# New SBUF addresses for the operands of the feed-forward matmuls in a fused attention and feed-forward kernel

## The chip, the cores and the metric

The kernel runs on one core of one Trainium2 chip, in one launch. The metric is the device time of that launch in microseconds. Before the change it is 646.93 us, the median of three runs (645.04, 646.93 and 648.34).

## What is computed

The reference is an attention layer followed by a two-layer feed-forward network, all in float32. Batch 4, 8 heads, 768 positions, head size 64; 3072 tokens of width 512, inner width 2048. Each query sees its neighbours at a distance below 16 and 24 block summaries (the maximum of the keys and the mean of the values of each block of 32 positions).

```python
k_sum = k.reshape(B, H, nb, block, D).max(axis=3)
v_sum = v.reshape(B, H, nb, block, D).mean(axis=3)
scores_all = concat([where(|i - j| < 16, scale * q @ k.T, -1e9), scale * q @ k_sum.T + log(block)])
attn = softmax(scores_all) @ concat([v, v_sum])
x = attn.transpose(0, 2, 1, 3).reshape(B * S, H * D)
h = x @ w_in
g = h * tanh(softplus(h))
out = g @ w_out
```

## The kernel before, in words

**Tiling.** The tokens are cut into 6 groups `g` of 512, the inner width into 16 blocks `fc` of 128. A pair (g, fc) is a step, 96 in all. Every float32 operand of the feed-forward part is kept as two numbers of type fp32r, an upper part (`hi`, `xh`, `ah`) and a rest (`lo`, `xl`, `al`), and a product is the sum of three: upper by upper, rest by upper, upper by rest.

**The feed-forward matmuls.** `ff_in` (L416, its matmul at L422) makes one 128x512 block of `h`: the stationary operand is a 128x128 slice of `w_in`, the moving one a 128x512 slice of `xh` or `xl`; 4 slices times 3 products are 12 matmuls a step. `ff_act` (L426) applies the activation on ScalarE, `ff_split` (L432) makes `ah` and `al`. `ff_out` (L442, its matmul at L450) has a 128x128 slice of `ah` or `al` as stationary operand and a 128x512 slice of `w_out` as moving one: 4 token tiles times 3 products, 12 matmuls a step, added up over the 16 blocks in four PSUM banks. That makes 96 x 24 = 2304 matmuls of 512 columns. Each has a weight load of its own for its stationary operand.

**Weights.** They arrive as raw 64-bit words, are made into `hi` and `lo` on ScalarE and VectorE in the first part of the run, and stay in SBUF. Blocks 0 to 9 are the `w_early` tiles, taken from the pool `const` (L98 to L103). Blocks 10 to 15 are the `w_late` tiles, taken after the pool `first_att` (L161) has been given back (L583).

**Attention.** It has units of 64 queries x 4 of a pair of heads. Its matmuls are in float32: scores (L312 to L318), transposes of the probabilities (L371, moving operand `ident`, stationary `pr`), products with the values (L398, moving operand `pt`, stationary `vw`), and at the start sums of values (L247, moving `vw` or `v`, stationary `blocks`). They stand between the steps.

**What sets the order.** The first part follows a written list of operations (`order`, L541 on), the rest a loop over the steps (L606 on): `ff_in` of step i, attention work, `ff_out` of step i - 2. TensorE takes all its work in this order.

**What sets the addresses.** A pool's tiles lie one behind the other in SBUF, the pools in the order in which they are opened. Addresses below are bytes from the start of a partition. A slice of a stationary operand begins a multiple of 512 bytes behind its tile's start, a slice of a moving operand a multiple of 2048 bytes.

Of the kernel before, what the change touches and what calls it, by code (L numbers as in the profile page):

```python
# [10 lines left out]
F32R = mybir.dt.float32r  # L11
# [9 lines left out]
P = 128  # L21
# [8 lines left out]
HP = H // 2  # L30
NCC = DM // P
NFC = DFF // P
# [7 lines left out]
EARLY = 10  # L40
NR = (S - TG) // P
NW = CG * NQ
WP = 512
# [14 lines left out]
def fused_kernel(ctx: ExitStack, tc: tile.TileContext, q0, qk, kt, v0, vw, vs, w_in, w_out, out):  # L58
    nc = tc.nc
    PS = bass.MemoryType.PSUM  # L60

    const = ctx.enter_context(tc.tile_pool(name="const", bufs=1))
    stage = ctx.enter_context(tc.tile_pool(name="stage", bufs=2))
    xp = ctx.enter_context(tc.tile_pool(name="xp", bufs=2))
    att = ctx.enter_context(tc.tile_pool(name="att", bufs=2))
    small = ctx.enter_context(tc.tile_pool(name="small", bufs=8))
    ff = ctx.enter_context(tc.tile_pool(name="ff", bufs=3))
    ps_o = ctx.enter_context(tc.tile_pool(name="ps_o", bufs=4, space=PS))

    ps_w = ctx.enter_context(tc.tile_pool(name="ps_w", bufs=4, space=PS))  # L70
# [9 lines left out]
    for h in range(2):  # L80
        r = slice(h * QT, (h + 1) * QT)
        nc.gpsimd.affine_select(
            out=base[r, 0:KW], in_=base[r, 0:KW], pattern=[[1, KW]], base=-1,
            channel_multiplier=-1, compare_op=ALU.is_ge, fill=NEG / SCALE)
        nc.gpsimd.affine_select(
            out=base[r, 0:KW], in_=base[r, 0:KW], pattern=[[-1, KW]], base=2 * WIN - 1,
# [8 lines left out]
    nc.gpsimd.memset(last[QT:P, KW - WIN:KW], NEG / SCALE)  # L95


    def weight_tiles(pool, name, blocks):  # L98
        return [[pool.tile([P, blocks, WP], F32R, name=f"{name}_{w}_{part}") for part in ("hi", "lo")]
                for w in ("in", "out")]  # L100

    early = weight_tiles(const, "w_early", EARLY)
    late = []  # L103

    def weight(w, part, fc):
# [52 lines left out]


    begin = ExitStack()  # L160
    first_att = begin.enter_context(tc.tile_pool(name="first_att", bufs=HP))  # L161

    blocks = first_att.tile([P, NW + NR, NB], F32, tag="blocks", name="blocks", bufs=1)
    nc.gpsimd.memset(blocks, 1.0 / BLK)
    for part, step, at0 in ((blocks[:, :NW], QT, -WIN), (blocks[:, NW:], P, TG)):
        n = part.shape[1]
        nc.gpsimd.affine_select(
            out=part, in_=part, pattern=[[step, n], [-BLK, NB]], base=at0, channel_multiplier=1,  # L170
            compare_op=ALU.is_ge, fill=0.0)
        nc.gpsimd.affine_select(
            out=part, in_=part, pattern=[[-step, n], [BLK, NB]], base=BLK - 1 - at0, channel_multiplier=-1,
            compare_op=ALU.is_ge, fill=0.0)
    part = blocks[:, :NW]
    nc.gpsimd.affine_select(
        out=part, in_=part, pattern=[[0, NW], [0, NB]], base=-WIN, channel_multiplier=1,
        compare_op=ALU.is_ge, fill=0.0)
    nc.gpsimd.affine_select(
        out=part, in_=part, pattern=[[0, NW], [0, NB]], base=WIN + QT - 1, channel_multiplier=-1,  # L180
# [384 lines left out]
    def parse(word):  # L565
        name = next(m for m in sorted(ops, key=len, reverse=True) if word.startswith(m))
        return name, word[len(name):]
# [10 lines left out]
    for k, word in enumerate(order):  # L578
        name, what = parse(word)
        ops[name](what)  # L580
        if k == end_of_begin:
            begin.close()
            late += weight_tiles(ctx.enter_context(tc.tile_pool(name="late", bufs=1)), "w_late", NFC - EARLY)  # L583


    done = 1 + max(int(word[2:]) for word in order if word.startswith("ph"))
# [19 lines left out]
    for i in range(done, len(steps) + 2):  # L606
# [24 lines left out]
        if i in transposes:  # L631
            home = ff.tile([P, WB * WP], F32, tag="f", name=f"pt_{i}", bufs=1)[0:KA]
# [48 lines left out]
```

## Time and profile before

| what | before |
|---|---|
| device time, median of 3 runs | 646.93 us (645.04 to 648.34) |
| span of the profiled execution, first to last instruction | 645.3 us |
| TensorE busy, share of the span | 626.7 us, 97% |
| TensorE weight loads busy | 510.5 us, 79% |
| VectorE / ScalarE / GpSimd busy | 288.8 / 270.5 / 75.0 us |

The profiled execution has no time of its own beside its span; the span lies between the lowest and the middle one of the three runs. Matmuls are pipelined: the record of one goes on after the next has started, so a busy TensorE is not TensorE at its peak, and the step from one start to the next is shorter than a record.

### The profile page before, as it was taken

The numbers are of one execution on the slowest core, as the hardware profiler recorded it, in microseconds if no ns is written. First come the engines' busy times: TensorE is split into PE (matmuls) and PEld (weight loads), VectorE is DVE, ScalarE is ACT, GpSimd is POOL, SyncE is SP. The second block draws the span as 40 slices with busy tenths as digits, with TensorE's granted clock in tenths as the row PEclk, the third lists the DMA queues.
The fourth block names the chain that finished last, engine by engine and source line by source line (L and its number), as shares of the span: only waits on it lengthen the run. The fifth ranks groups of instructions, "written<-read, shape, count | busy, mean of one in ns | idle before, by whom it ended". The sixth has DMA issues, their size and how long they took to land.

```text
span 645.3 us, 10991 instructions
## 1 busy us (share of the span) xinstructions
PE 626.7 (97%) x4272; PEld 510.5 (79%) x4272; DVE 288.8 (45%) x817; ACT 270.5 (42%) x659; POOL 75.0 (12%) x119
## 2 busy tenths in 40 slices
PE   4799899999999999999999999999999999999997
PEld 3687788777888888888888888888888888888886
DVE  4899999993222445423223444332332232222211
ACT  4887678583433425415424434244244251111111
POOL 4432121220101001001001010010010010000000
PEclk9999999999999999999999999999999999999999
DMA  8978656642202234603202254233132010100001
GB/s 263 243 263 287 211 216 202 226 163 93 67 27 93 73 121 113 216 1 95 63 33 93 91 153 125 86 95 94 66 94 81 15 32 1 65 1 0 1 0 66
DMA packets 31780, 68.24 MB, mean 106 GB/s; under 512 B 6768, under 2 KB 11632, under 8 KB 31728
## 3 DMA queue, kind: packets, MB, share of 16 engines
q1 hardware_dynamic: 31728, 67.53, 33.2%
q8 instruction: 34, 0.56, 0.4%
q14 instruction: 18, 0.15, 0.1%
HBM read 59.11 MB, written 6.29 MB: 101 GB/s over the span
## 4 chain that ended last, share of the span: by engine, by line
PE 80%; DVE 6%; ACT 1%; issue 1%; DVEq 0%
PE po L450 37%; PE ph L422 36%; PE x_ps L398 3%; PE sc L312 2%; PE pt_ps L371 2%; DVE w L140 1%; DVE al L440 1%; DVE w L136 1%; DVE w_f L144 1%; DVE w_f L149 1%; DVE w_early_out_lo L157 1%; ACT pr L345 0%; DVE vq L260 0%; DVE km L239 0%; DVE pr L334 0%
## 5 line engine op out<-in xcount | busy, mean ns | idle before, releaser
L429 ACT ACTIVATE a<-ph 128x512 f32<-128x512 f32 x96 | 57.2, 597 | 250.5 <-PE ph L422 166.6
L438 DVE CAST ah<-a 128x512 fp32r<-128x512 f32 x80 | 34.1, 426 | 239.1 <-ACT a L429 237.7
L365 POOL TENSOR_TENSOR pr<-pr,rs 128x480 f32<-128x480 f32 x48 | 54.8, 1143 | 362.2 <-DVE rs L361 297.3
L450 PE MATMUL po<-w_early_out_hi,ah 128*128 128x512 f32 x240 | 96.6, 402 | 0.0
L450 PE MATMUL po<-w_early_out_hi,al 128*128 128x512 f32 x240 | 95.1, 396 | 0.1
L422 PE MATMUL ph<-xh,w_early_in_hi 128*128 128x512 f32 x240 | 95.1, 396 | 0.0
L450 PE MATMUL po<-w_early_out_lo,ah 128*128 128x512 f32 x240 | 94.6, 394 | 0.0
L422 PE MATMUL ph<-xh,w_early_in_lo 128*128 128x512 f32 x240 | 94.0, 392 | 0.0
L422 PE MATMUL ph<-xl,w_early_in_hi 128*128 128x512 f32 x240 | 93.6, 390 | 0.0
L345 ACT ACTIVATE pr<-pr,nm 128x120 f32<-128x120 f32 x192 | 73.3, 384 | 9.5 <-DVE nm L334 9.3
L440 DVE TENSOR_TENSOR al<-a,ah 128x512 fp32r<-128x512 f32 x96 | 68.1, 710 | 4.0 <-ACT ah L438 1.3
L422 PE MATMUL ph<-xh,w_late_in_hi 128*128 128x512 f32 x144 | 57.6, 400 | 0.0
L450 PE MATMUL po<-w_late_out_hi,ah 128*128 128x512 f32 x144 | 57.2, 397 | 0.0
L422 PE MATMUL ph<-xh,w_late_in_lo 128*128 128x512 f32 x144 | 57.0, 396 | 0.1
L422 PE MATMUL ph<-xl,w_late_in_hi 128*128 128x512 f32 x144 | 56.8, 394 | 0.0
L450 PE MATMUL po<-w_late_out_lo,ah 128*128 128x512 f32 x144 | 56.3, 391 | 0.0
L450 PE MATMUL po<-w_late_out_hi,al 128*128 128x512 f32 x144 | 56.2, 390 | 0.0
L450 PEld LDWEIGHTS po<-w_early_out_hi,ah 128*128 128x128 f32 x240 | 45.2, 188 | 11.6 <-issue 1.9
L450 PEld LDWEIGHTS po<-w_early_out_lo,ah 128*128 128x128 f32 x240 | 45.3, 189 | 10.6
L450 PEld LDWEIGHTS po<-w_early_out_hi,al 128*128 128x128 f32 x240 | 45.3, 189 | 10.4 <-DVE al L440 0.5
L422 PEld LDWEIGHTS ph<-xh,w_early_in_lo 128*128 128x128 f32 x240 | 45.1, 188 | 10.0
L422 PEld LDWEIGHTS ph<-xl,w_early_in_hi 128*128 128x128 f32 x240 | 45.2, 188 | 9.5
(77 smaller groups left out, 828.7 us busy)
## 6 DMA issues: line engine op xcount, KB each, us to landing
qk<-qk SPq DMA_DIRECT2D x40, 496.0 KB
w<-w_in SPq DMA_DIRECT2D x16, 512.0 KB
w<-w_out SPq DMA_DIRECT2D x16, 512.0 KB
vw<-vw SPq DMA_DIRECT2D x40, 192.0 KB
ks<-kt SPq DMA_DIRECT2D x16, 384.0 KB
out<-o SPq DMA_DIRECT2D x24, 256.0 KB
vsum<-vs SPq DMA_DIRECT2D x12, 384.0 KB
vw<-vm SPq DMA_DIRECT2D x40, 48.0 KB
```

Source lines behind the costliest of these rows:

```text
L136: nc.vector.tensor_scalar(out=x, in0=x, scalar1=29, scalar2=None, op0=ALU.logical_shift_right)
L140: nc.vector.scalar_tensor_tensor(out=x, in0=high, scalar=SIGN, in1=x, op0=ALU.bitwise_and, op1=ALU.bitwise_or)
L312: nc.tensor.matmul(ps[h][row, at0:at0 + KA], u["qk"][r, s, h * QT:(h + 1) * QT], u["qk"][r, s, P:], start=True, stop=True)
L345: nc.scalar.activation(pr[:, s, :], pr[:, s, :], AF.Exp, scale=-1.0, bias=nm[:, s:s + 1], accum_out=sm[:, s:s + 1])
L365: nc.gpsimd.tensor_mul(u["p"], u["p"], u["r"].unsqueeze(2).broadcast_to([P, NQ, KA]))
L371: nc.tensor.transpose(ps[:KA, s * P:(s + 1) * P], u["p"][:, s, :], ident)
L398: nc.tensor.matmul(x, u["v"][0:rows, s, d], pt, start=(c >= CG), stop=(c >= CG or s == NQ - 1))
L422: nc.tensor.matmul(ph, w[:, cc * P:(cc + 1) * P], x[:, cc, :], start=(cc == 0 and n == 0), stop=(cc == NCC - 1 and n == 2))
L429: nc.scalar.activation(a, st[g, fc], AF.Mish)
L438: (nc.scalar.copy if g == 0 else nc.vector.tensor_copy)(ah, a)
L440: return lambda: nc.vector.tensor_sub(al, a, ah.bitcast(F32))
L450: nc.tensor.matmul(po[g][t], a[:, tok], w, start=(fc == 0 and n == 0), stop=(fc == NFC - 1 and n == 2))
```

## The change

No operation, size or order changes. The pools get other places: `pool(name, bufs, side)` takes a pool's memory from the low end of SBUF (`left`) or from the high end (`right`). `ff` (with `ah`, `al`) and `const` (with `w_early_in`) come first from the low end; `xp` (`xh`, `xl`) and a new pool `moving` (with `w_early_out`) first from the high end.

```diff
-    const = ctx.enter_context(tc.tile_pool(name="const", bufs=1))
-    stage = ctx.enter_context(tc.tile_pool(name="stage", bufs=2))
-    xp = ctx.enter_context(tc.tile_pool(name="xp", bufs=2))
-    att = ctx.enter_context(tc.tile_pool(name="att", bufs=2))
-    small = ctx.enter_context(tc.tile_pool(name="small", bufs=8))
-    ff = ctx.enter_context(tc.tile_pool(name="ff", bufs=3))
+    def pool(name, bufs, side):
+        return ctx.enter_context(tc.tile_pool(name=name, bufs=bufs, side=side))
+
+    ff = pool("ff", 3, "left")
+    const = pool("const", 1, "left")
+    xp = pool("xp", 2, "right")
+    moving = pool("moving", 1, "right")
+    stage = pool("stage", 2, "right")
+    att = pool("att", 2, "right")
+    small = pool("small", 8, "right")
...
-    early = weight_tiles(const, "w_early", EARLY)
+    early = weight_tiles((const, moving), "w_early", EARLY)
...
-    first_att = begin.enter_context(tc.tile_pool(name="first_att", bufs=HP))
+    first_att = begin.enter_context(tc.tile_pool(name="first_att", bufs=HP, side="left"))
...
-            late += weight_tiles(ctx.enter_context(tc.tile_pool(name="late", bufs=1)), "w_late", NFC - EARLY)
+            late += weight_tiles([pool("late", 1, "left")] * 2, "w_late", NFC - EARLY)
```

`weight_tiles` takes one pool for `w_in` and one for `w_out`. In the two built programs the tiles of the feed-forward part begin here (bytes in the partition):

| tile | role | before | changed |
|---|---|---|---|
| w_early_in_hi, _lo | stationary in `ff_in` | 3104, 23584 | 23584, 44064 |
| w_late_in_hi, _lo | stationary in `ff_in` | 180128, 192416 | 64544, 76832 |
| xh (2 buffers) | moving in `ff_in` | 105504, 113696 | 196576, 204768 |
| xl (2 buffers) | moving in `ff_in` | 121888, 130080 | 212960, 221152 |
| ah (3 buffers) | stationary in `ff_out` | 167840, 169888, 171936 | 9344, 11392, 13440 |
| al (3 buffers) | stationary in `ff_out` | 173984, 176032, 178080 | 15488, 17536, 19584 |
| w_early_out_hi, _lo | moving in `ff_out` | 44064, 64544 | 155616, 176096 |
| w_late_out_hi, _lo | moving in `ff_out` | 204704, 216992 | 89120, 101408 |
| vw (2 buffers) | stationary at L398 | 152480, 154528 | 128736, 130784 |
| pt (first list / loop) | moving at L398 | 156576 / 159648 | 132832 / 1152 |
| ident | moving at L371 | 1152 | 21632 |

## Rows read from the trace of the kernel before

**Rows 1.** The page: span, and busy time by engine (share of the span, instructions).

```profile
span 645.3 us, 10991 instructions
PE 626.7 (97%) x4272; PEld 510.5 (79%) x4272; DVE 288.8 (45%) x817; ACT 270.5 (42%) x659; POOL 75.0 (12%) x119
```

**Rows 2.** The page's 40 slices: granted TensorE clock in tenths.

```profile
PEclk9999999999999999999999999999999999999999
```

**Rows 3.** The page: chain that ended last, by engine and by line.

```profile
PE 80%; DVE 6%; ACT 1%; issue 1%; DVEq 0%
PE po L450 37%; PE ph L422 36%; PE x_ps L398 3%; PE sc L312 2%; PE pt_ps L371 2%; DVE w L140 1%; DVE al L440 1%; DVE w L136 1%; DVE w_f L144 1%; DVE w_f L149 1%; DVE w_early_out_lo L157 1%; ACT pr L345 0%; DVE vq L260 0%; DVE km L239 0%; DVE pr L334 0%
```

**Rows 4.** Costliest groups, feed-forward matmuls: busy us, mean ns of one, idle before.

```profile
L450 PE MATMUL po<-w_early_out_hi,ah 128*128 128x512 f32 x240 | 96.6, 402 | 0.0
L450 PE MATMUL po<-w_early_out_hi,al 128*128 128x512 f32 x240 | 95.1, 396 | 0.1
L422 PE MATMUL ph<-xh,w_early_in_hi 128*128 128x512 f32 x240 | 95.1, 396 | 0.0
L450 PE MATMUL po<-w_early_out_lo,ah 128*128 128x512 f32 x240 | 94.6, 394 | 0.0
L422 PE MATMUL ph<-xh,w_early_in_lo 128*128 128x512 f32 x240 | 94.0, 392 | 0.0
L422 PE MATMUL ph<-xl,w_early_in_hi 128*128 128x512 f32 x240 | 93.6, 390 | 0.0
...
L422 PE MATMUL ph<-xh,w_late_in_hi 128*128 128x512 f32 x144 | 57.6, 400 | 0.0
L450 PE MATMUL po<-w_late_out_hi,ah 128*128 128x512 f32 x144 | 57.2, 397 | 0.0
L422 PE MATMUL ph<-xh,w_late_in_lo 128*128 128x512 f32 x144 | 57.0, 396 | 0.1
L422 PE MATMUL ph<-xl,w_late_in_hi 128*128 128x512 f32 x144 | 56.8, 394 | 0.0
L450 PE MATMUL po<-w_late_out_lo,ah 128*128 128x512 f32 x144 | 56.3, 391 | 0.0
L450 PE MATMUL po<-w_late_out_hi,al 128*128 128x512 f32 x144 | 56.2, 390 | 0.0
```

**Rows 5.** Timeline of PE, first matmul of six steps: start us, length us, instruction.

```profile
399.20 0.40 PE L450 MATMUL po<-w_early_out_hi,ah 128*128 128x512 f32 x1
...
401.99 0.40 PE L422 MATMUL ph<-xh,w_early_in_hi 128*128 128x512 f32 x1
...
404.75 0.40 PE L450 MATMUL po<-w_early_out_hi,ah 128*128 128x512 f32 x1
...
421.84 0.39 PE L422 MATMUL ph<-xh,w_late_in_hi 128*128 128x512 f32 x1
...
424.62 0.39 PE L450 MATMUL po<-w_late_out_hi,ah 128*128 128x512 f32 x1
...
427.34 0.39 PE L422 MATMUL ph<-xh,w_late_in_hi 128*128 128x512 f32 x1
```

**Rows 6.** Groups, 244.594 to 244.6 us: last matmul before a step of w_early_in.

```profile
L450 PE MATMUL po<-w_late_out_lo,ah 128*128 128x512 f32 x1 | 0.4, 397 | 0.0
```

**Rows 7.** Groups, 325.97 to 325.98 us: last matmul before a step of w_late_in.

```profile
L450 PE MATMUL po<-w_late_out_lo,ah 128*128 128x512 f32 x1 | 0.4, 389 | 0.0
```

**Rows 8.** Groups by line, attention matmuls, the whole span.

```profile
L398 PE MATMUL x_ps<-pt,vw 120*64 120x64 f32 (+1 forms) x768 | 28.8, 225 | 1.8 <-DMA vw<-vm 1.8
L247 PE MATMUL vm_ps<-v,blocks 128*24 128x128 f32 x16 | 2.4, 272 | 0.0
```

**Rows 9.** Groups by line, transposes, 200 to 640 us.

```profile
L371 PE MATMUL pt_ps<-ident,pr 128*120 128x128 f32 x112 | 14.5, 272 | 0.0
```

More of the change, by code (lines that the diff above doesn't have):

```diff
@@ L95, in fused_kernel, with weight_tiles @@
     nc.gpsimd.memset(last[QT:P, KW - WIN:KW], NEG / SCALE)
-    def weight_tiles(pool, name, blocks):
-        return [[pool.tile([P, blocks, WP], F32R, name=f"{name}_{w}_{part}") for part in ("hi", "lo")]
-                for w in ("in", "out")]
-    early = weight_tiles(const, "w_early", EARLY)
+    def weight_tiles(pools, name, blocks):
+        return [[home.tile([P, blocks, WP], F32R, name=f"{name}_{w}_{part}") for part in ("hi", "lo")]
+                for w, home in zip(("in", "out"), pools)]
+    early = weight_tiles((const, moving), "w_early", EARLY)
     late = []
```

## Prediction

> **What bounds the kernel now.** I read the page from the top: busy time, clock, chain, groups. TensorE is busy for 97% of the span [rows 1], its granted clock is full in every slice [rows 2], which is the 2.4 GHz level, and the chain that ended last is TensorE for 80%, with 73% on two lines, `po` L450 and `ph` L422 [rows 3]. So the 2304 feed-forward matmuls set the time, and a nanosecond on each is worth 2.3 us. ScalarE, VectorE and GpSimd are busy for less than half [rows 1]; what they do at new addresses lies beside TensorE's work.
>
> A record is longer than the step to the next start, so I first ask whether differences between records are differences in time. A step of twelve `w_early_out` matmuls runs from 399.20 to 401.99, 2.79 us or 232.5 ns each; one of `w_late_out` from 424.62 to 427.34, 2.72 us or 226.7 ns [rows 5]. The records of these groups have means of 402, 396 and 394 ns against 397, 390 and 391 [rows 4]: 397.3 and 392.7 on average. Both kinds of record are some 165 ns longer than the step, so the difference carries over: 5 to 6 ns by starts, 4.7 by records.
>
> **The change part by part.** No instruction is added, dropped or moved: on each of the five engines the changed program has the same operations in the same order with the same waits. Only addresses differ, so the question is what an address costs. The trace holds the answer in part, for the four kinds of feed-forward matmul are equal in shape and differ in where their operands lie [rows 4]:
>
> - `ff_in`, early weights: moving above stationary, records 396, 392, 390 ns (720 matmuls).
> - `ff_in`, late weights: moving below, 400, 396, 394 (432).
> - `ff_out`, early weights: moving below, 402, 396, 394 (720).
> - `ff_out`, late weights: moving above, 397, 390, 391 (432).
>
> Same line, same products, same engine: the pairs with the moving operand above are 4 ns faster in `ff_in` and 3 to 6 ns in `ff_out`. Read so, the order of the two addresses decides, and the change would put all 2304 on the fast side.
>
> But the four pairs differ in something else too. Take the tiles' starts modulo 512 bytes; slices keep these remainders. Early `ff_in`: stationary 3104 = 6 x 512 + 32, moving 105504 = 206 x 512 + 32: equal. Late `ff_out`: 167840 leaves 416, 204704 leaves 416: equal. Early `ff_out`: 416 against 32 (44064). Late `ff_in`: 416 (180128) against 32. So the two fast kinds are also the two with equal remainders. Order and remainder can't be told apart by these four groups.
>
> One place tells them apart. The load of the next stationary operand runs while a matmul streams, so the neighbour counts too. The last matmul of a late `ff_out` step moves `w_late_out_lo` (remainder 416, start 216992) while the first weights of the next step are loaded. If these are `w_late_in_hi` (180128, remainder 416), its record is 389 ns [rows 7]; if they are `w_early_in_hi` (3104, remainder 32), it is 397 ns [rows 6]. In both the moving operand lies above both stationary ones. By order both should be fast; by remainder the second is slow, as it is. The run has 10 places of the slow sort, all 396 or 397, and 12 of the fast sort, all 389 or 390. I therefore take the remainder as what decides, and the order as a companion of it.
>
> Now the changed homes. Early `ff_in`: 23584 leaves 32, 196576 leaves 480. Late `ff_in`: 64544 leaves 32, against 480. Early `ff_out`: 9344 leaves 128, 155616 leaves 480. Late `ff_out`: 128 against 32 (89120). No pair is equal any more, so the two fast kinds become slow and the two slow ones stay:
>
> - early `ff_in`: 240 x ((400 - 396) + (396 - 392) + (394 - 390)) = 240 x 12 ns = +2.9 us;
> - late `ff_out`: 144 x ((402 - 397) + (396 - 390) + (394 - 391)) = 144 x 14 ns = +2.0 us.
>
> Sum +4.9 us. The first and last starts give less: a late `ff_in` step takes 424.62 - 421.84 = 2.78 us against 404.75 - 401.99 = 2.76, so 60 x 0.02 + 36 x (2.79 - 2.72) = +3.7 us [rows 5]; these are single steps, and I take the means. The new differences (448, 352, 448 and 416 modulo 512) are not among those that the trace has as slow (128, and 384 at the seam). What such a difference costs is bounded below by the fast rows, nothing lost anywhere and 240 x 14 + 144 x 12 ns = 5.1 us won, and above by the slowest row, 402 ns for every matmul: 240 x (6 + 6 + 8 + 10 + 12) + 144 x (2 + 5 + 6 + 8 + 11 + 12) ns = +16.4 us, 663 us. The nearest rows are the unequal ones, each kind against its own line, and I take those; the far end would need every matmul to do as badly as the slowest of twelve groups does, and I leave it to the 2 in 10 outside.
>
> The attention matmuls move too. At L398 the loop's `pt` comes to lie below `vw` and at another remainder. If each of the 768 passes [rows 8] lost 5 ns, that would be 3.8 us. I take nothing: the transposes have the moving operand below the stationary one and unequal remainders, the value sums of `v` have it above, with 128 columns both, and both records are 272 ns [rows 8, 9]. At the other end there is no gain, as these pairs are aligned and in order now.
>
> The sum is made against the profiled execution, 645.3 + 4.9 = 650.2 us of span; the median of the runs stands 1.6 us above that span, so 646.9 + 4.9 = **651.8 us**.
>
> **The rivals.** *Order decides after all.* Then late `ff_in` and early `ff_out` take the fast values, -(240 x 14 + 144 x 12) ns = -5.1 us: 641.8 us, faster. For it: all four groups [rows 4]. Against it: the seam [rows 6, 7], which it must lay to something else, a far jump of the stationary address, say. If that jump alone makes the seam slow, order has it. Chance 0.20.
>
> *Only certain differences hurt.* If unequal remainders cost time only at 128 and 384, the new ones are harmless, and the time is the same 641.8 us. Nothing in the trace speaks for it or against it. Chance 0.10.
>
> *Above, but not too far.* Fast pairs lie 25088 to 131584 bytes apart, the slow seam 220032. The changed early pairs are 134080 to 202176 apart. If these are too far already, early `ff_in` turns slow, late `ff_out` stays fast and no other kind gains: +2.9, 649.8 us, which counts as no change. Chance 0.08.
>
> *Addresses don't matter*, and early and late differ by something that stays. Then nothing changes: 646.9 us. Against it, the same late weights are slow in `ff_in` and fast in `ff_out` [rows 4], so it is not lateness. The Trainium skill, SBUF — State Buffer, "Who interferes with whom", says that TensorE reads the moving operand and the weights through two independent ports and waits for nobody; by that rule the sum would be 0 and not +4.9. The trace disagrees with it by 3 to 6 ns per matmul. With partial effects that cancel, chance 0.12.
>
> **How the numbers follow.** My forecast, all unequal pairs slow, has 0.50; its own range is 650.2 (the +3.7, less 0.4 of scatter) to 653.4 (1.6 us of scatter, about what the runs show, above 651.8). The range must hold 8 in 10, so it has to go through "no change" (0.20) and into the faster cases (0.30): 641.0 to 653.4 takes in most of those at 641.8. Three runs can tell a change of about 0.5% from none, 3.2 us here, so slower begins at 650.2 and faster ends at 643.7. Faster 0.20 + 0.10 = 0.30, same 0.08 + 0.12 = 0.20, slower 0.50.
>
> **What would show it.** Right: in the groups of the changed kernel all twelve feed-forward rows stand at 394 to 402 ns, early `ff_in` up by 4 and late `ff_out` by 3 to 6, steps of 2.78 us and more everywhere, the clock still full, the chain's shares unchanged. Wrong by order or by harmless remainders: all twelve at 390 to 397 ns and steps of about 2.72 us. Wrong by distance: late `ff_out` alone at 390 to 397. The attention lines show the omitted term: L398 above 225 ns would put it into the sum.

## The result, and the profile after

The changed kernel takes 650.02 us (median of 11 runs, 648.94 to 651.39) against 645.99 us for the kernel before on the same chips (11 runs, 644.24 to 648.34). The ratio is 1.0066, with a 95% interval of 1.0051 to 1.008: slower by 4.0 us, where 4.9 was forecast.

The page of the changed kernel: span and busy time, clock, chain.

```profile
span 648.8 us, 10991 instructions
PE 632.0 (97%) x4272; PEld 510.0 (79%) x4272; DVE 288.5 (44%) x817; ACT 270.4 (42%) x659; POOL 74.6 (12%) x119
...
PEclk9899999999999999999999999999999999999999
...
PE 91%; DVE 4%; DMA 1%; ACT 1%; issue 1%; POOL 1%; SPq 1%; POOLq 0%
```

Against [rows 1 to 3]: TensorE is busy for 632.0 us where it was 626.7; the other engines are as they were. Lines have moved by 4: L422 is now L426, L450 is L454. The chain runs through TensorE for 91% instead of 80%. The two shares don't cover the same stretch: the chain of the kernel before was followed back to 67.5 us only, this one to the start. One early slice has a clock a tenth lower; that part did not take longer, as the starts further down show.

The groups of the changed kernel, which answer to [rows 4]:

```profile
L454 PE MATMUL po<-w_early_out_hi,ah 128*128 128x512 f32 x240 | 96.3, 401 | 0.0
L426 PE MATMUL ph<-xh,w_early_in_hi 128*128 128x512 f32 x240 | 95.7, 399 | 0.0
L454 PE MATMUL po<-w_early_out_hi,al 128*128 128x512 f32 x240 | 95.3, 397 | 0.0
L426 PE MATMUL ph<-xl,w_early_in_hi 128*128 128x512 f32 x240 | 94.8, 395 | 0.0
L426 PE MATMUL ph<-xh,w_early_in_lo 128*128 128x512 f32 x240 | 94.7, 394 | 0.0
L454 PE MATMUL po<-w_early_out_lo,ah 128*128 128x512 f32 x240 | 94.5, 394 | 0.0
...
L454 PE MATMUL po<-w_late_out_hi,ah 128*128 128x512 f32 x144 | 57.7, 401 | 0.0
L426 PE MATMUL ph<-xh,w_late_in_hi 128*128 128x512 f32 x144 | 57.7, 400 | 0.0
L454 PE MATMUL po<-w_late_out_hi,al 128*128 128x512 f32 x144 | 57.0, 396 | 0.0
L454 PE MATMUL po<-w_late_out_lo,ah 128*128 128x512 f32 x144 | 57.0, 396 | 0.0
L426 PE MATMUL ph<-xl,w_late_in_hi 128*128 128x512 f32 x144 | 56.9, 395 | 0.0
L426 PE MATMUL ph<-xh,w_late_in_lo 128*128 128x512 f32 x144 | 56.8, 395 | 0.0
```

Early `ff_in` went from 396, 390, 392 ns (`hi` by `xh`, `hi` by `xl`, `lo`) to 399, 395, 394, late `ff_out` from 397, 390, 391 (`hi` by `ah`, by `al`, `lo`) to 401, 396, 396. The two kinds that were slow stayed within 1 ns. For the two kinds that rose this is 240 x (3 + 5 + 2) + 144 x (4 + 6 + 5) ns = 2.4 + 2.2 = 4.6 us.

The starts of the first and the last feed-forward matmul say the same. Timeline of PE, kernel before:

```profile
46.75 0.50 PE L422 MATMUL ph<-xh,w_early_in_hi 128*128 128x512 f32 x1
...
641.06 0.39 PE L450 MATMUL po<-w_late_out_lo,ah 128*128 128x512 f32 x1
```

The same of the changed kernel:

```profile
45.38 0.50 PE L426 MATMUL ph<-xh,w_early_in_hi 128*128 128x512 f32 x1
...
644.57 0.40 PE L454 MATMUL po<-w_late_out_lo,ah 128*128 128x512 f32 x1
```

From first to last it was 594.31 us and is 599.19, 4.88 us more. The part ahead of it was 1.37 us shorter in this execution, which is why the spans differ by only 3.5 us. That first stretch moves about from profile to profile (45.07 to 48.47 us over the kernels below), so the stretch from first to last is the cleaner measure of what the matmuls cost.

### The profile page after: what moved, and what is told of

Its sections match the earlier page's. It is cut to its first block, busy times and chain, and to the rows that moved or that the text cites. A ratio compares the mean times of both kernels' runs of the same rounds, so it can differ in the third digit from the quotient of the medians.

```text
span 648.8 us, 10991 instructions
## 1 busy us (share of the span) xinstructions
PE 632.0 (97%) x4272; PEld 510.0 (79%) x4272; DVE 288.5 (44%) x817; ACT 270.4 (42%) x659; POOL 74.6 (12%) x119
## 4 chain that ended last, share of the span: by engine, by line
PE 91%; DVE 4%; DMA 1%; ACT 1%; issue 1%; POOL 1%; SPq 1%; POOLq 0%
PE po L454 41%; PE ph L426 39%; PE x_ps L402 3%; PE pt_ps L375 3%; PE sc L316 3%; PE vm_ps L251 1%; ACT pr L349 1%; POOL pr L369 1%; DMA vw<-vm 1%; DVE w_f L153 1%; PE sc L320 1%; DMA q<-qk 0%; DVE w L140 0%; DVE w_f L148 0%; DVE w L144 0%
## 5 line engine op out<-in xcount | busy, mean ns | idle before, releaser
L454 PE MATMUL po<-w_early_out_hi,ah 128*128 128x512 f32 x240 | 96.3, 401 | 0.0
L426 PE MATMUL ph<-xh,w_early_in_hi 128*128 128x512 f32 x240 | 95.7, 399 | 0.0
L454 PE MATMUL po<-w_early_out_hi,al 128*128 128x512 f32 x240 | 95.3, 397 | 0.0
L426 PE MATMUL ph<-xl,w_early_in_hi 128*128 128x512 f32 x240 | 94.8, 395 | 0.0
L426 PE MATMUL ph<-xh,w_early_in_lo 128*128 128x512 f32 x240 | 94.7, 394 | 0.0
L454 PE MATMUL po<-w_early_out_lo,ah 128*128 128x512 f32 x240 | 94.5, 394 | 0.0
L454 PE MATMUL po<-w_late_out_hi,ah 128*128 128x512 f32 x144 | 57.7, 401 | 0.0
L426 PE MATMUL ph<-xh,w_late_in_hi 128*128 128x512 f32 x144 | 57.7, 400 | 0.0
L454 PE MATMUL po<-w_late_out_hi,al 128*128 128x512 f32 x144 | 57.0, 396 | 0.0
L454 PE MATMUL po<-w_late_out_lo,ah 128*128 128x512 f32 x144 | 57.0, 396 | 0.0
L426 PE MATMUL ph<-xl,w_late_in_hi 128*128 128x512 f32 x144 | 56.9, 395 | 0.0
L426 PE MATMUL ph<-xh,w_late_in_lo 128*128 128x512 f32 x144 | 56.8, 395 | 0.0
L454 PEld LDWEIGHTS po<-w_early_out_hi,ah 128*128 128x128 f32 x240 | 45.0, 188 | 12.4 <-issue 1.9
L426 PEld LDWEIGHTS ph<-xh,w_early_in_lo 128*128 128x128 f32 x240 | 45.1, 188 | 10.9
L454 PEld LDWEIGHTS po<-w_early_out_lo,ah 128*128 128x128 f32 x240 | 45.1, 188 | 10.8
L426 PEld LDWEIGHTS ph<-xh,w_early_in_hi 128*128 128x128 f32 x240 | 45.1, 188 | 10.5
L426 PEld LDWEIGHTS ph<-xl,w_early_in_hi 128*128 128x128 f32 x240 | 45.1, 188 | 10.3
```

The source lines that it names most:

```text
L426: nc.tensor.matmul(ph, w[:, cc * P:(cc + 1) * P], x[:, cc, :], start=(cc == 0 and n == 0), stop=(cc == NCC - 1 and n == 2))
L454: nc.tensor.matmul(po[g][t], a[:, tok], w, start=(fc == 0 and n == 0), stop=(fc == NFC - 1 and n == 2))
```

## The experiments

All start from the kernel before, but for the second one. Each moves tiles, some with a few unused bytes added, and changes no operation; the time of the kernel before on the same chip was between 645.98 and 646.25 us. Differences of addresses are modulo 256 unless said otherwise.

### Equal remainders, order as before

```diff
+    kms = ctx.enter_context(tc.tile_pool(name="kms", bufs=HP, side="right"))
...
-        km = att.tile([P, NB], F32, tag="km", name=f"km{b}_{hp}", bufs=HP)
+        km = kms.tile([P, NB], F32, tag="km", name=f"km{b}_{hp}", bufs=HP)
```

> The kernel before, with the four km tiles (384 bytes) taken from the high end of SBUF: ff and late move down by 384 bytes, so that all tiles of the feed-forward part leave 32 modulo 512. Order as before: early ff_in and late ff_out have the moving operand above, early ff_out and late ff_in below. Remainder theory: all twelve groups at 390 to 397 ns, 5.1 us less than before, about 640.9 us. Order theory: early ff_out and late ff_in stay at 394 to 402 ns, time as before, 646.0 us. If addresses don't matter: as before.

Measured: 640.01 us, ratio to the kernel before 0.9902 (0.9885 to 0.9918). Its groups:

```profile
L451 PE MATMUL po<-w_early_out_hi,ah 128*128 128x512 f32 x240 | 95.3, 397 | 0.0
L423 PE MATMUL ph<-xh,w_early_in_hi 128*128 128x512 f32 x240 | 94.4, 393 | 0.0
L451 PE MATMUL po<-w_early_out_hi,al 128*128 128x512 f32 x240 | 93.7, 390 | 0.4 <-DVE al L441 0.3
L451 PE MATMUL po<-w_early_out_lo,ah 128*128 128x512 f32 x240 | 93.6, 390 | 0.0
L423 PE MATMUL ph<-xl,w_early_in_hi 128*128 128x512 f32 x240 | 93.5, 389 | 0.0
L423 PE MATMUL ph<-xh,w_early_in_lo 128*128 128x512 f32 x240 | 93.4, 389 | 0.0
...
L451 PE MATMUL po<-w_late_out_hi,ah 128*128 128x512 f32 x144 | 57.0, 396 | 0.0
L423 PE MATMUL ph<-xh,w_late_in_hi 128*128 128x512 f32 x144 | 56.8, 395 | 0.0
L423 PE MATMUL ph<-xh,w_late_in_lo 128*128 128x512 f32 x144 | 56.2, 390 | 0.4 <-DVE w_late_in_lo L158 0.4
L451 PE MATMUL po<-w_late_out_lo,ah 128*128 128x512 f32 x144 | 56.1, 390 | 0.0
L451 PE MATMUL po<-w_late_out_hi,al 128*128 128x512 f32 x144 | 56.1, 390 | 0.0
L423 PE MATMUL ph<-xl,w_late_in_hi 128*128 128x512 f32 x144 | 56.1, 389 | 0.0
```

All twelve lie between 389 and 397 ns, early `ff_out` and late `ff_in` too, although their moving operand still lies below. The four kinds no longer differ. Moving 384 bytes out of the way wins 1%; the order has no part in it.

### Moving operand above, equal remainders

```diff
+    kms = pool("kms", HP, "right")
+    first_mask = pool("first_mask", 1, "right")
     xp = pool("xp", 2, "right")
...
     small = pool("small", 8, "right")
+    masks = pool("masks", 1, "right")
...
-    base = const.tile([P, KA], F32, name="base")
+    base = first_mask.tile([P, KA], F32, name="base")
...
-    first = const.tile([P, KA], F32, name="first")
+    first = masks.tile([P, KA], F32, name="first")
...
-    last = const.tile([P, KA], F32, name="last")
+    last = masks.tile([P, KA], F32, name="last")
```

This diff is against the changed kernel; `km` comes from `kms` as above.

> The changed kernel with km and one mask put above xp and two masks below small, so that every feed-forward tile leaves 128 modulo 512; the moving operand stays above the stationary one everywhere, as far away as in the changed kernel. Remainder theory: all twelve groups at 390 to 397 ns, about 640.9 us. Order theory: as in the changed kernel, since the order is the same, 650.0 us. Distance theory (slow from some distance between 131584 and 220032 bytes): early ff_in and early ff_out stay at 394 to 402 ns, near 647 to 650 us.

Measured: 638.89 us, ratio 0.988 (0.9865 to 0.9895). The groups of early `ff_in`, whose operands lie further apart (from 134656 bytes on) than any fast pair of the kernel before (up to 131584):

```profile
L429 PE MATMUL ph<-xh,w_early_in_hi 128*128 128x512 f32 x240 | 94.5, 394 | 0.0
...
L429 PE MATMUL ph<-xh,w_early_in_lo 128*128 128x512 f32 x240 | 93.5, 390 | 0.0
L429 PE MATMUL ph<-xl,w_early_in_hi 128*128 128x512 f32 x240 | 93.4, 389 | 0.0
```

Against the changed kernel's 399, 394 and 395: same order, same distances to within 1.5 KB, only the remainders made equal, and 11 us less. Order and distance are both out. The runs can't tell whether it is faster than the first experiment (638.89 against 640.01 us, runs that overlap); with two of the runs below (639.45 and 639.94 us) these are the fastest arrangements found.

### A difference of 256

```diff
-    small = ctx.enter_context(tc.tile_pool(name="small", bufs=8))
+    small = ctx.enter_context(tc.tile_pool(name="small", bufs=8, side="right"))
```

Against the first experiment.

> As the first run, with small (768 bytes) also taken from the high end: early ff_out and late ff_in differ by 256 modulo 512, early ff_in and late ff_out are equal. If equal remainders modulo 256 suffice: all twelve groups at 390 to 397 ns, about 640.9 us. If it takes 512: early ff_out and late ff_in at 394 to 402 ns, 646.0 us. Order theory: also 646.0 us.

Measured: 639.45 us, ratio 0.9889 (0.9875 to 0.9904). Early `ff_out`, whose operands differ by 256:

```profile
L451 PE MATMUL po<-w_early_out_hi,ah 128*128 128x512 f32 x240 | 95.3, 397 | 0.0
...
L451 PE MATMUL po<-w_early_out_hi,al 128*128 128x512 f32 x240 | 93.8, 391 | 0.6 <-DVE al L441 0.3
L451 PE MATMUL po<-w_early_out_lo,ah 128*128 128x512 f32 x240 | 93.5, 390 | 0.0
```

As with equal remainders. So it is 256 bytes that count and not 512, which the prediction had used.

### A difference of 32

```diff
+    shift = ctx.enter_context(tc.tile_pool(name="shift", bufs=1)).tile([P, 8], F32, name="shift")
     ff = ctx.enter_context(tc.tile_pool(name="ff", bufs=3))
```

Against the first experiment.

> As the first run, with 32 bytes put ahead of ff: early ff_out and late ff_in differ by 32 modulo 512, the other two are equal. If any difference costs: early ff_out and late ff_in at 394 to 402 ns, 646.0 us. If only differences of 64 bytes or more cost: all twelve at 390 to 397 ns, about 640.9 us. Order theory: 646.0 us.

Measured: 647.21 us, ratio 1.0008 (0.9992 to 1.0025). Early `ff_out`:

```profile
L452 PE MATMUL po<-w_early_out_hi,ah 128*128 128x512 f32 x240 | 96.4, 402 | 0.0
L452 PE MATMUL po<-w_early_out_hi,al 128*128 128x512 f32 x240 | 95.0, 396 | 0.1
L452 PE MATMUL po<-w_early_out_lo,ah 128*128 128x512 f32 x240 | 95.0, 396 | 0.0
```

A tile of 32 bytes ahead of `ff` takes the whole gain back: 397, 390, 390 become 402, 396, 396, and the time is that of the kernel before, which has a difference of 128 here.

Early `ff_in` has equal pairs here, but its last `lo` matmul streams while the load of `ah`, 32 off, begins. One such place, 403.645 to 403.7 us:

```profile
L424 PE MATMUL ph<-xh,w_early_in_lo 128*128 128x512 f32 x1 | 0.4, 397 | 0.0
```

In all 42 steps in which `ff_out` follows directly, this record is 397 ns; in the first experiment it is 389 in all 42. So an unequal next load costs 8 ns at a difference of 32.

### Own pair or next load

```diff
     ff = ctx.enter_context(tc.tile_pool(name="ff", bufs=3))
+    rest = ctx.enter_context(tc.tile_pool(name="rest", bufs=3, side="right"))
...
-        al = ff.tile([P, TG], F32R, tag="al", name=f"al{g}_{fc}")
+        al = rest.tile([P, TG], F32R, tag="al", name=f"al{g}_{fc}")
```

Against the first experiment.

> The kernel of the first run, but al lies alone at the high end with remainder 96 modulo 256 where ah and both w_out lie at 32. In ff_out a matmul of (hi, ah) then has its own pair equal and the load of the next stationary operand (al) unequal; (hi, al) has its own pair unequal and the next load (ah) equal; (lo, ah) has both equal. If both the own pair and the next load count: (hi, ah) and (hi, al) some 5 ns above the first run's 397 and 390 (396 and 390 for late), (lo, ah) at 390; 768 x 5 ns = 3.8 us above the first run's 640.0, 643.8 us. If only the own pair counts: (hi, al) alone slow, 641.9 us. If only the next load counts: (hi, ah) alone slow, 641.9 us. ff_in as in the first run.

Measured: 645.14 us, ratio 0.9977 (0.9958 to 0.9996). Early `ff_out`, `al` off by 64:

```profile
L452 PE MATMUL po<-w_early_out_hi,ah 128*128 128x512 f32 x240 | 95.5, 398 | 0.0
L452 PE MATMUL po<-w_early_out_hi,al 128*128 128x512 f32 x240 | 95.4, 398 | 0.0
...
L452 PE MATMUL po<-w_early_out_lo,ah 128*128 128x512 f32 x240 | 93.5, 389 | 0.0
```

The (hi, al) group, whose own pair is unequal, rose by 8 ns; the (hi, ah) group, during which the unequal `al` is loaded, by 1 (late: 396 to 398). This is none of the three cases as written: the matmul with the unequal `al` is slow, the one during its load hardly. The time rose by 5.1 us, more than the 384 x 8 + 384 x 2 ns = 3.8 us of the groups. From the first to the last feed-forward matmul it is 4.2 us more than in the first experiment (591.57 against 587.33). The rest lies ahead of them: in the profiled execution the first one started at 48.47 us, 3.4 us later than in the first experiment. There a batch of four value sums of `v` (L249) takes 1.06 us at 24.80 us and one of the same shape 0.60 at 28.09; in the first experiment it is 0.60 already at 20.43. Two lengths of one kind of instruction in one execution speak against the address of `al`; the granted clock of this stretch reads full, so what made them long stays open. The ten runs lie in two bunches, 642.8 to 643.4 and 644.8 to 646.1.

### Own pair or next load, off by 128

```diff
+    ctx.enter_context(tc.tile_pool(name="shift", bufs=1, side="right")).tile([P, 16], F32, name="shift")
+    rest = ctx.enter_context(tc.tile_pool(name="rest", bufs=3, side="right"))
     att = ctx.enter_context(tc.tile_pool(name="att", bufs=2))
     kms = ctx.enter_context(tc.tile_pool(name="kms", bufs=HP, side="right"))
```

Against the first experiment, with `al` from `rest` as above.

> As the run in which al alone differed, but al now lies 128 off the others modulo 256 and not 64 (160 against 32). There the own pair cost 7 to 8 ns ((hi, al) 398 against 390) and the next load 1 to 2 ((hi, ah) 398 against 397, late 398 against 396). In the kernel before, at the seam, the next load alone cost 7 ns at a difference of 128 (397 against 389 or 390). If the price of the next load depends on the difference: (hi, ah) near 402 to 404 here, (hi, al) slow too, (lo, ah) at 390. If the seam's cost was something of the step boundary: (hi, ah) at 398 as there.

Measured: 642.56 us, ratio 0.9943 (0.992 to 0.9965). Early `ff_out`:

```profile
L453 PE MATMUL po<-w_early_out_hi,ah 128*128 128x512 f32 x240 | 96.5, 402 | 0.0
L453 PE MATMUL po<-w_early_out_hi,al 128*128 128x512 f32 x240 | 95.4, 397 | 0.4 <-DVE al L443 0.3
...
L453 PE MATMUL po<-w_early_out_lo,ah 128*128 128x512 f32 x240 | 93.6, 390 | 0.0
```

Now both rise, (hi, ah) by 5 and (hi, al) by 7 ns, and (lo, ah) stays. The means hold a few records of some 500 ns; medians leave them out. Lowest, median and highest record, from the views by line: (hi, ah) of the first experiment, with `al` 64 off, with `al` 128 off, and last (hi, al) with `al` 128 off.

```profile
L451 PE MATMUL po<-w_early_out_hi,ah x240: 388/389/504, 56.1 to 604.8; 128*128 128x512 f32 x120
...
L452 PE MATMUL po<-w_early_out_hi,ah x240: 388/392/502, 59.5 to 612.0; 128*128 128x512 f32 x120
...
L453 PE MATMUL po<-w_early_out_hi,ah x240: 388/396/505, 56.5 to 608.6; 128*128 128x512 f32 x120
L453 PE MATMUL po<-w_early_out_hi,al x240: 390/397/504, 56.7 to 608.9; 128*128 128x512 f32 x120
```

So the load of the next stationary operand has a price of its own, and it depends on the difference without growing with it: 8 ns at 32 (above), 3 at 64, 7 at 128. The seam of [rows 6, 7], 397 against 389 ns at 128, is this effect and needs no step boundary. From the first to the last feed-forward matmul this run is 3.9 us above the first experiment (591.18 us), its median 2.6 us above.

The matmul with the unequal `al` costs 8 ns more at either difference. That this is the price of its own pair is not shown, for it also comes right behind the unequal load. At the seam the two can be parted: the matmul behind it has an equal pair and an equal next load, and is slow all the same. Kernel before, 244.84 to 244.99 us:

```profile
L422 PE MATMUL ph<-xh,w_early_in_hi 128*128 128x512 f32 x1 | 0.4, 393 | 0.0
```

It is 393 or 394 ns at all 10 seams of this sort, and 389 in the first experiment. Some 4 of the 8 ns may thus be an after-effect of the load. Nor do the prices add up. In early `ff_out` of the kernel before, pair and next load are both 128 off:

```profile
L450 PE MATMUL po<-w_early_out_hi,ah x240: 390/395/505, 57.8 to 613.0; 128*128 128x512 f32 x120
L450 PE MATMUL po<-w_early_out_hi,al x240: 387/393/504, 58.0 to 613.3; 128*128 128x512 f32 x120
```

That is 4 to 6 ns above 389, less than either price alone.

### A difference of 16

```diff
...
+        t = alone.tile([P, blocks * WP + 8], F32R, name=name)
+        return t[:, 4:4 + blocks * WP].rearrange("p (k f) -> p k f", f=WP)
...
```

For `w_early_in_hi`, which gets a pool `alone` at the high end, behind 32 unused bytes; against the first experiment.

> The kernel of the first run, but w_early_in_hi lies alone at the high end, 16 bytes off the common remainder (48 against 32 modulo 256). If 16 bytes are enough: the three groups of early ff_in rise from 393, 389 and 389 ns by 3 to 5 ns (own pair of the hi products, next load for lo), 720 x 4 ns = 2.9 us above the first run, about 642.9 us. If they are not enough: as the first run, 640.0 us. Late ff_in and ff_out as in the first run in both cases.

Measured: 639.94 us, ratio 0.9909 (0.9876 to 0.9942). Early `ff_in`:

```profile
L431 PE MATMUL ph<-xh,w_early_in_hi 128*128 128x512 f32 x240 | 94.6, 394 | 0.0
...
L431 PE MATMUL ph<-xh,w_early_in_lo 128*128 128x512 f32 x240 | 93.5, 390 | 0.0
L431 PE MATMUL ph<-xl,w_early_in_hi 128*128 128x512 f32 x240 | 93.5, 390 | 0.0
```

Within 1 ns of the first experiment's 393, 389 and 389, and the same time: a difference of 16 bytes costs nothing, one of 32 does.

## Why the prediction was right, point by point

**The bound.** TensorE's two feed-forward lines set the time before and after; the busy times of the other engines are the same to within half a microsecond.

**The cause.** The four groups alone [rows 4] fitted order and remainder alike. The one place that parted them, the seam [rows 6, 7], was read rightly: equal remainders make the pairs fast with the moving operand below (first experiment) and above (second), and unequal ones make them slow with it above (the changed kernel). The order of the addresses was a companion, not the cause.

**The terms.** Early `ff_in` was forecast at +2.9 us and measured at +2.4 by its records, late `ff_out` at +2.0 and +2.2; the two kinds that should stay did. The change is 4.6 us by these records, 4.88 by the stretch from the first to the last feed-forward matmul and 4.0 by the medians; that the forecast of 4.9 meets the second of these to the last digit is luck. In the profiled execution the stretch ahead was 1.37 us shorter, and the forecast had it unchanged; whether that holds for the other runs is not shown. The forecast level of 651.8 us lies 1.8 us above the 650.02 measured: 0.9 from the change, and 0.9 because the kernel before takes 645.99 us over eleven runs and not 646.93.

**The range, and the rival by distance.** The range, 641.0 to 653.4 us, ran from "faster" through "no change" to "slower", so that the time lies in it says little. 650.02 us lies just under the range of the forecast's own case, which began at 650.2, and 0.2 us from the 649.8 of the rival by which the changed early pairs lie too far apart. The time alone doesn't part these two. The groups do: by that rival late `ff_out` stays fast, and it rose by 4 to 6 ns; and the second experiment has early pairs as far apart, all fast. (Its 649.8 was a little high: by its own distances some late `ff_in` pairs, from 109504 bytes apart, would have turned fast, worth under 1 us.) Of the signs named, the twelve rows came, at 394 to 401 ns; the chain's shares did not stay, and the clock was a tenth lower in one slice.

**The unknown differences.** Nothing in the trace told what 192, 96 and 160 modulo 256 would cost. Taking the nearest unequal rows held: 394 to 401 ns. The rival by which only certain differences hurt fell for this change, but has a true part: differences of 256 and 16 cost nothing.

**The attention matmuls.** Nothing was taken for them, and nothing came. The transposes of [rows 9] are 272 ns over the same stretch again. The group at L402 of the changed kernel, against 225 ns in [rows 8]:

```profile
L402 PE MATMUL x_ps<-pt,vw 120*64 120x64 f32 (+1 forms) x768 | 28.8, 225 | 1.7 <-DMA vw<-vm 1.7
```

**The rival without any effect.** The Trainium skill, SBUF — State Buffer, "Who interferes with whom", gives TensorE two independent read ports and says that it waits for nobody. By the runs the time does depend on the addresses: kernels that differ in them alone lie 11 us apart, 638.89 and 650.02 us, and each difference tried from 32 to 192 bytes modulo 256 (32, 64, 96, 128, 160, 192) has a cost. Whether the cost is a wait at a port is not shown.

**What was too small.** For the fast side the prediction had 5.1 us. Equal remainders won 6.2 and 7.4 us by the medians (first and second experiment, each against its 646.25), because the two kinds that were fast before gained as well: early `ff_in` went from 396, 390 and 392 ns to 393, 389 and 389. Part of that is the seam: the last `lo` matmul of a step is followed directly by the load of `ah` in 42 of 60 steps (160 against 32 modulo 256). Its record is 396 or 397 ns there and 389 in the first experiment, and the group's mean carried this price as if it belonged to the fast level. That is 42 x 7.5 ns = 0.3 us; the 10 seams behind late `ff_out` and the matmuls that follow these seams add some 0.15. The rest was not taken apart.

## What to carry to other kernels

Where matmuls follow each other without a gap, look at the SBUF addresses of the stationary and the moving operand modulo 256 bytes, the next stationary operand included: equal remainders were worth 4 to 8 ns of some 230 for each 512-column fp32r matmul in this kernel. A few small tiles in the pools between two large ones decided this, so it is worth trying to put small tiles at the other end of SBUF and to keep the sizes between large tiles at multiples of 256 bytes; no other kernel was tried. And where two explanations fit all large groups of a profile, look for the few instructions at a seam on which they differ.

## What the runs showed of the hardware that was not expected

The price of an unequal remainder is not one number. Against a median of 389 ns where all is equal, a matmul during which an unequal stationary operand is loaded takes 8 ns more at a difference of 32, 3 at 64 and 7 at 128; the matmul that uses this operand takes 8 more at 64 and at 128; and where every pair is 128 off, a matmul takes 4 to 6 more and not the sum. A difference of 16 bytes costs nothing and one of 32 as much as one of 128 (402, 396, 396 ns against 402, 396, 394). What in the memory does this was not tried, nor whether differences between 16 and 32 bytes matter; operands of other types were seen only in the attention matmuls, which have 256 columns at most and showed nothing at the addresses that they had.
